# A new list of step order and step engines for a linear-attention and SoLU feed-forward kernel on one Trainium2 core

## The chip, the core and the metric

The kernel runs on one core of a Trainium2 chip, in one launch. The metric is the device time of that launch in microseconds. The inputs are drawn once; q, k and v are 8 batches of 8 heads, 576 rows and 64 columns in float32, the weights are 512 by 1024 and 1024 by 512, and the output is 4608 by 512.

## The reference

```python
q_s = softmax(q, axis=-1)                 # over a head's 64 columns
k_s = softmax(k, axis=2)                  # over the 576 rows of the sequence
kv  = einsum('bhsd,bhse->bhde', k_s, v)
x   = einsum('bhsd,bhde->bhse', q_s, kv)  # then heads side by side: 4608 x 512
h   = x @ w_in
sm  = softmax(h, axis=-1)
solu = h * sm
ln  = (solu - mean) / sqrt(var + 1e-6) * g_ln
out = ln @ w_out
```

## The kernel before

The work is cut into named streams, each a Python generator. One call of a stream emits one step: one instruction or a few, on engines that the code fixes or, where the code says `on(default)`, on an engine that the list can choose. A constant, ORDER (L21 to L85), is the whole schedule: a string of names, and `in_turns` (L643) calls the streams in the order of the string. The n-th mention of a name is that stream's n-th step, counted here from 0, so h1[14] is the fifteenth mention of h1. `*3` repeats a name, `.v` asks for VectorE. In a step without `on(...)` the suffix does nothing. Each engine executes its instructions in the order in which the string emits them, and an instruction that waits holds up all that stands behind it on its engine; the DMA queue of SyncE, which carries every transfer, works the same way.

The streams, with their lines:

- LQ, LK, LV, V: loads of q, k and v of a batch (L177 to L218). V has a second step that casts to the tile with a column of ones (L190, ScalarE or VectorE).
- w0 to w3 and y0 to y3: the rows of w_in and w_out. Two loads of 512 KB, then L239 (ScalarE), L241 and L243 (VectorE) which turn the 64-bit words into float32, then a sum of magnitudes (L256 or L287, ScalarE). W and Z then scale the weights and split them into two float16 parts: W[0] to W[3] find the scale of w_in, W[4] to W[11] are L268 on ScalarE and L270 on VectorE in turn; Z does the same for w_out, with L309 and L311, Z[0] being L292 to L297 and Z[19] the last L311.
- K of a batch (L335): maxima over rows (L346, L348, L351 on VectorE; transposes L322 and L329 on TensorE), subtraction (L357, L362, chosen), Exp (L359, L364), the product with v (L376, L381), the scale (L384 to L390, L157, L164 to L168) and the float16 block matrix (L403 to L407).
- Q..a, Q..c, R (L412 to L478): softmax of q (L424, L426, L428, L431 to L435, L437), a split into two float16 parts (L440, L442) and a transposing DMA.
- x of a row tile (L494): 16 or 32 small matmuls, then L516 on ScalarE and L518 on VectorE.
- h of a row tile (L522): 24 matmuls of 512 columns in six steps (L533), L540 and L542, Exp (L546), four one-column operations am, pi, p, ph (L550 to L559, GpSimd by default), the product with its sum (L562 on VectorE, L564), u (L567 on ScalarE, L569 on VectorE), the transposing DMA (L572), the square (L576, ScalarE) and four more one-column operations (L580 to L589).
- o of a row tile (L594): 24 matmuls in four steps (L607), the copy out of the accumulator (L615 on VectorE or L617 on ScalarE), the store.
- P: four matmuls on zeros (L662), whose result nobody reads.

There are 36 row tiles. The accumulator of h has two buffers, so the matmuls of one tile can start only after L576 of the tile two before it; o has one buffer, and x, K and the scales share three. TensorE's order is a mix: steps of h, o, x and K stand between each other as the string says.

Of the kernel before, what the change touches and what calls it, by code (L numbers as in the profile page):

```python
# [17 lines left out]
P = 128  # L18

BUFS = 12, 4, 2  # L20
ORDER = (  # L21
# [63 lines left out]
)  # L85


@with_exitstack
def linear_attention_solu_ffn(ctx: ExitStack, tc: tile.TileContext, q, k, v, w_in, w_out, g_ln, out):

# [633 lines left out]
```

## Time and profile before

| quantity | value |
|---|---|
| time of the runs, median of 3 | 489.39 us (489.34 to 490.88) |
| span of the profiled execution, first to last instruction | 488.0 us |
| TensorE, busy share of the span | 93% |
| VectorE | 74% |
| ScalarE | 57% |
| GpSimd | 42% |
| mean granted clock of TensorE | 0.972 |
| DMA, mean | 154 GB/s |

The profiled execution's own time is not listed apart from its span; against the median of the runs the span is 1.39 us shorter. A busy TensorE is not TensorE at its peak, because matmuls overlap; its useful work is better counted in matmuls.

### The profile page before, as it was taken

The numbers are of one execution on the slowest core, as the hardware profiler recorded it, in microseconds if no ns is written. First come the engines' busy times: TensorE is split into PE (matmuls) and PEld (weight loads), VectorE is DVE, ScalarE is ACT, GpSimd is POOL, SyncE is SP. The second block draws the span as 40 slices with busy tenths as digits, with TensorE's granted clock in tenths as the row PEclk, the third lists the DMA queues.
The fourth block names the chain that finished last, engine by engine and source line by source line (L and its number), as shares of the span: only waits on it lengthen the run. The fifth ranks groups of instructions, "written<-read, shape, count | busy, mean of one in ns | idle before, by whom it ended". The sixth has DMA issues, their size and how long they took to land.

```text
span 488.0 us, 8325 instructions
## 1 busy us (share of the span) xinstructions
PE 453.0 (93%) x3150; PEld 223.0 (46%) x3150; DVE 359.2 (74%) x610; ACT 280.2 (57%) x463; POOL 202.7 (42%) x303
## 2 busy tenths in 40 slices
PE   5748576999999999999999999999999999999997
PEld 1324242445555444454445445544554444444444
DVE  3989999987889897887897885987786754544220
ACT  1577698777648546765574656654645544533322
POOL 3312666478526636742564457254231431221120
PEclk9868987999999999999999999999999999999999
DMA  8899589279875967569659947794225544151162
GB/s 263 274 208 297 205 178 219 63 151 249 198 194 128 247 105 172 135 147 253 131 130 217 246 100 164 140 253 103 66 43 109 107 109 88 39 113 19 47 152 84
DMA packets 159240, 74.99 MB, mean 154 GB/s; under 512 B 127840, under 2 KB 152672, under 8 KB 159200
## 3 DMA queue, kind: packets, MB, share of 16 engines
q1 hardware_dynamic: 159200, 74.47, 64.4%
q8 instruction: 24, 0.39, 0.3%
q14 instruction: 16, 0.13, 0.1%
HBM read 36.70 MB, written 9.44 MB: 95 GB/s over the span
## 4 chain that ended last, share of the span: by engine, by line
PE 78%; DVE 12%; ACT 4%; DMA 3%; issue 2%; SPq 0%; POOL 0%; DVEq 0%; ACTq 0%
PE o L607 36%; PE h L533 34%; PE x L509 3%; PE kv L376 3%; DMA kr<-in_k_dram 2%; DVE u L569 2%; DVE top L540 1%; DMA v<-in_v_dram 1%; DVE wi L270 1%; ACT u L567 1%; DVE gw L243 1%; DVE h L562 1%; ACT e L576 1%; DVE qnmx L424 1%; PE kv L381 1%
## 5 line engine op out<-in xcount | busy, mean ns | idle before, releaser
L533 PE MATMUL h<-wi,xT 128*128 128x512 f16 x864 | 203.9, 385 | 11.2 <-ACT e L576 9.8
L607 PE MATMUL o<-wo,uT 128*128 128x512 f16 (+1 forms) x888 | 197.7, 373 | 0.8 <-DVE os L615 0.8
L533 PEld LDWEIGHTS <-xT 128*128 128x128 f16 x864 | 84.2, 99 | 111.6 <-issue 18.5
L607 PEld LDWEIGHTS <-uT 128*128 128x128 f16 x888 | 85.3, 98 | 96.7 <-issue 1.1
L540 DVE TENSOR_REDUCE top<-h 128x1 f32<-128x1024 f32 x36 | 43.9, 1219 | 43.3 <-PE h L533 43.3
L569 DVE SCALAR_TENSOR_TENSOR u<-h,nmu,u 128x1024 f16<-128x1024 f32 x36 | 45.9, 1276 | 15.0 <-ACT u L567 14.9
L576 ACT ACTIVATE e<-h,nmu 128x1024 f32<-128x1024 f32 x36 | 40.0, 1111 | 20.9 <-DVE u L569 20.8
L562 DVE SCALAR_TENSOR_TENSOR h<-h,ph,e 128x1024 f32<-128x1024 f32 x36 | 46.2, 1283 | 7.2 <-POOL ph L559 6.2
L542 ACT ACTIVATE nm<-top,hs 128x1 f32<-128x1 f32 x32 | 9.4, 294 | 61.8 <-DVE top L540 61.8
L567 ACT ACTIVATE u<-h,nmu 128x1024 f16<-128x1024 f32 x36 | 40.0, 1111 | 1.0
L442 POOL TENSOR_TENSOR qhl<-qm,qhl 128x1024 f16<-128x1024 f32 (+1 forms) x12 | 24.9, 2075 | 34.9 <-ACT qhl L148 22.0
L546 ACT ACTIVATE e<-h,nm,hs 128x1024 f32<-128x1024 f32 x32 | 38.4, 1200 | 0.8
L556 POOL TENSOR_TENSOR p<-pi,mone 128x1 f32<-128x1 f32 x36 | 22.6, 627 | 37.9 <-DVE pi L553 36.5
L550 POOL TENSOR_SCALAR am<-nm 128x1 f32<-128x1 f32 x17 | 7.6, 449 | 70.0 <-ACT nm L542 69.9
L426 POOL TENSOR_TENSOR qm<-qm,qnmx 128x1024 f32<-128x1024 f32 (+1 forms) x14 | 25.1, 1799 | 24.0 <-DVE qnmx L424 20.5
L437 POOL TENSOR_TENSOR qm<-qm,qrec 128x1024 f32<-128x1024 f32 (+1 forms) x13 | 24.8, 1911 | 12.9 <-DVE qrec L435 6.7
L589 POOL TENSOR_TENSOR r<-var,mhalf 128x1 f32<-128x1 f32 x36 | 20.3, 565 | 23.9 <-DVE var L586 23.2
L564 ACT ACTIVATE nmu<-s 128x1 f32<-128x1 f32 x36 | 7.3, 202 | 38.3 <-DVE h L562 35.1
L518 DVE SCALAR_TENSOR_TENSOR xT<-x,xT 128x512 f16<-128x512 f32 x36 | 24.3, 679 | 3.2 <-ACT xT L516 3.2
L615 DVE TENSOR_SCALAR os<-o,rr 128x512 f32<-128x512 f32 (+1 forms) x18 | 12.9, 719 | 17.9 <-PE o L607 17.6
L509 PEld LDWEIGHTS <-bd 128*64 128x64 f16 x640 | 18.3, 113 | 15.7 <-issue 11.6
L617 ACT ACTIVATE os<-o,rr 128x512 f32<-128x512 f32 x19 | 13.0, 683 | 18.6 <-PE o L607 14.2
(130 smaller groups left out, 564.0 us busy)
## 6 DMA issues: line engine op xcount, KB each, us to landing
v<-in_v_dram SPq DMA_DIRECT2D x32, 256.0 KB, 3.9
out_dram<-os SPq DMA_DIRECT2D x31, 256.0 KB, 3.0
km<-in_k_dram SPq DMA_DIRECT2D x7, 1024.0 KB, 6.6
qm<-in_q_dram SPq DMA_DIRECT2D x7, 1024.0 KB, 6.2
w_in<-in_moe_w_in_dram SPq DMA_DIRECT2D x8, 512.0 KB, 5.8
w_out<-in_moe_w_out_dram SPq DMA_DIRECT2D x8, 512.0 KB, 5.6
out_dram<-os SPq DMA_DIRECT2D x10, 128.0 KB, 2.4
qm<-in_q_dram SPq DMA_DIRECT2D x2, 512.0 KB, 4.3
```

The source lines that it names most:

```text
L426: on(nc.gpsimd).tensor_tensor(x, x, wide(nmx), op=ALU.add)
L437: on(nc.gpsimd).tensor_tensor(x, x, wide(rec), op=ALU.mult)
L442: on(nc.gpsimd).tensor_tensor(lo, x, hi, op=ALU.subtract)
L509: nc.tensor.matmul(acc[j * D : (j + 1) * D, pr, cols], t[:, s, 2 * pr + j], qT[:, 2 * pr + j, cols], start=(s == 0), stop=(s == 1),)
L533: nc.tensor.matmul(h[:, ns], xT[:, t, kc], wi[:, s, kc, ns], start=(i == 0), stop=(i == len(terms) - 1))
L540: nc.vector.tensor_reduce(top, h, axis=AX.X, op=ALU.max, negate=True)
L546: nc.scalar.activation(e, h, AF.Exp, bias=nm, scale=hs, accum_out=z)
L562: nc.vector.scalar_tensor_tensor(h, h, ph, e, op0=ALU.mult, op1=ALU.mult, accum_out=s1)
L567: nc.scalar.activation(u[:, 0], h, AF.Identity, bias=nmu)
L569: nc.vector.scalar_tensor_tensor(u[:, 1], h, nmu, u[:, 0], op0=ALU.add, op1=ALU.subtract)
L576: nc.scalar.activation(e, h, AF.Square, bias=nmu, accum_out=s2)
L607: nc.tensor.matmul(o, uT[:, j, f], wo[:, s, f, cols], start=(f == 0 and j == 0 and s == 0), stop=(f == NF - 1 and j == 1))
```

## The change

Only ORDER is replaced. Buffers, tiles, operations and their number stay; both lists hold the same 1728 steps, and every stream has the same number of mentions. What changes is the order in which the steps are emitted, and which engine a choosable step takes. The new list was searched with a model that limits the transfers in flight and counts the collisions of GpSimd and VectorE.

The suffix `.v` stands 163 times in the old list and 661 times in the new one, but most of the added ones are on steps that cannot choose. Counted by engine, the choosable steps that differ most are:

| step | before | after |
|---|---|---|
| copy of o: L617 ScalarE / L615 VectorE | 19 / 18 | 25 / 12 |
| cast of v (L190): ScalarE / VectorE | 21 / 11 | 24 / 8 |
| q minus its maximum, whole (L426): GpSimd / VectorE | 12 / 3 | 14 / 1 |
| q times the reciprocal, whole (L437): GpSimd / VectorE | 12 / 3 | 11 / 4 |
| k minus its maximum (L357): GpSimd / VectorE | 7 / 9 | 8 / 8 |
| am (L550), pi (L553), first z (L580) on GpSimd | 17, 18, 18 | 19, 20, 23 |
| second z (L583), var (L586) on GpSimd | 20, 21 | 16, 20 |

The heads of the two lists:

```diff
-    "LQ0*2 LK0*3 V03 w3 Q0a K0*4 Q0a*2 K0 P*4 K0 Q0b w3 V00 V03.v K0 Q0c K0 Q0b Q0a w3 w0 K0 w3 V00 Q0b "
-    "w3 V01 K0.v Q0b K0 w0 V01.v K0.v w0*2 LV0 K0 w0 K0.v Q0c*2 V02 w3 Q0a.v V02 w2 K0 w2 P*3 K0 Q0a.v "
-    "Q0b P*2 K0 w2 w1 Q0b w0 w1 K0 w2 Q0c Q0a Q0b K0*2 w2 K0 w1 K0 w1 K0*2 w1 K0 Q0a w2 LK1 Q0b K0*2 w1 "
-    "K0 Q0c.v V11 LK1 K1 P x0 x1 W K1 W y0 Q0c V12 K1 y1 W V11 x0 W x0 W Q0c K1 P h0 W*4 h0 K1 y0 h0 Q0c "
-    "W*2 h0 y1 W LQ1 y0 V10 S0.v h0*2 V12 y0 V13 K1 x1 h0 K1 x1 h0 x2 y0 h0 K1 y1 h1 x3 K1 y2 y1 h1 y2 "
-    "x2 h0 h1 x3 h1 h0 h0.v y0 h0 x2 K1 Q1a h0*4 h1 Q1c h1 y1 K1 y3 K1*2 LV1 y3 h2 Q1a*2 V10 h2 K1 V13 "
-    "h2 h1 h2 Q1a LQ1 h2 h1 Q1a.v h2 h1.v LQ1 K1 h0 y2 h1 K1*2 x3 Q1a K1 h1 h2*2 h1 y1 y2 h1 LG y3 Q1a "
-    "K1 h1 y2 K1 V21 K1 h2 Q1a y3 h1 LK2 h1 K1 h1 h2 h3 y2 h2*2 K1*2 h2 y3 K1 h3 h2 h1 y3 K1 h2 Z h3 K1 "
...
+    "LQ0*2 Q0a.v LK0 Q0b Q0a Q0b.v LK0 V03 K0*2 Q0a LK0 K0 w3 V03 K0 w3 Q0a P Q0b P K0 V00.v P Q0a Q0c.v "
+    "P w3 K0*3 Q0b.v w0*2 V00 V01 w3 Q0c K0 w3 w0 V01 K0.v w0 K0 K0.v K0 Q0c Q0a w0 Q0a K0.v Q0c V02 LV0 "
+    "V02 Q0b.v K0*2 w2 K0 Q0c.v K0 Q0b w2 V11 w2 K0 w1 K0 w0 Q0b w1 w2 w1 K0*2 Q0a LK1 Q0b.v w2 K0 P w1 "
+    "K0 K0.v K0*2 LK1 K0 w2 w1 K1 w3 w1 K1*2 V13 K1 W y1 x0 P W K1 Q0c W K1 x0 Q0c y1 V13 W K1 x1 x0 W*5 "
+    "K1 W*3 LG y1 y0 h0.v h0 y0 h0.v y1 h0 y0 h0 S0 h0 P K1 y0 Q0c x1 x3 V11 x2 h0 y0 h0 h0.v y0 x1 LQ1 "
+    "h0 P V10 h1 h0 x3 h1*2 LQ1 h0 x2 V10 Q1a K1 h1 V12 y2 h1 h0 y2 y1 Q1a h0 LV1 h0.v LV2 y3*2 h1 K1 V12 "
+    "K1 h0.v x2 h0 P y2 Q1c Q1a h1.v LQ1 K1 x3 Q1a y2 h1 K1 y3 h1 h2.v h2*3 K1 h1*2 h2 V22.v h2 Q1a.v Q1a "
+    "y1 K1*2 V21.v K1 h1 Q1c P h1*2 Q1a h2 K1*2 h1.v Q1a LK2 h2.v h1.v h2 K1 h1 P h2 h3 y2 h2.v y2 h3 "
...
```

Decoded for VectorE, between W[3] (the scale of w_in is known) and h1[14] (L569 of tile 1):

- Only the old list has there: K1[3] (L348), K1[4] (L351), S0 (L485), ph of tile 0 (L559), am of tile 1 (L550), y2[4] (L243), K1[20] (L157), y3[3] (L241). The first two stand ahead of W[3] in the new list, S0 and the two one-column operations are on GpSimd there, and the last three come after h1[14].
- Only the new list has there: am of tile 0 (L550).

From W[3] on to Z[19], only the old list has K1[3], K1[4], S0, ph of tile 0, am of tile 1, K2[2] (L346), K2[3] (L348), K2[4] (L351) and R1[0] (L424 on the rest of q); only the new list has am and the second z of tile 0.

On GpSimd, the old list has K1[9] (L357) behind p of tile 0 while ph of tile 0 stands on VectorE; the new list has ph of tile 0 ahead of K1[9], both on GpSimd. On TensorE, the order of streams up to h3 holds the same work; five of the eleven P steps stand ahead of K0's product with v in the old list after the first four, and none in the new one, which has P steps behind h0, x2, h1, K1[17] and K1[19] instead. On SyncE, the load V11 stands ahead of w1's loads in the new list and far behind them in the old one.

Between the last step of a tile's h and the first of the tile that takes over its accumulator, the new list has the least TensorE work at these places: h30 to h32 (24 matmuls of h31, 18 of o25), h26 to h28 (24 of h25, 18 of o20, K7[5]), h12 to h14 (24 of h13, 12 of o8, two x, K4[5] and K4[7]), h24 to h26 (24 of h22, 24 of o17), h11 to h13 and h31 to h33. In the old list the least is at h15 to h17 (24 of h16, 6 of o9, two x).

120 rows, old and new, of the table ORDER are left out of this document.

## The prediction, made before the change was run

> **What bounds the kernel now.** I read the page first, for the stretches that are not full.
>
> ```profile
> span 488.0 us, 8325 instructions
> PE 453.0 (93%) x3150; PEld 223.0 (46%) x3150; DVE 359.2 (74%) x610; ACT 280.2 (57%) x463; POOL 202.7 (42%) x303
> PE   5748576999999999999999999999999999999997
> DVE  3989999987889897887897885987786754544220
> ```
>
> The fortieths are 12.2 us long. TensorE (PE) is full from the eighth on, from about 85 us; before that VectorE (DVE) is full and TensorE is not. Two waits views, TensorE from 85 to 485 us and VectorE from 41 to 85 us, say how full (us in total, times, longest):
>
> ```profile
> PE h L533 <- ACT e L576: 1.7, 3, 0.9
> PE o L607 <- DVE os L615: 0.8, 1, 0.8
> ```
>
> ```profile
> DVE u L569 <- ACT u L567: 0.9, 1, 0.9
> DVE gw L241 <- ACT gw L239: 0.4, 1, 0.4
> ```
>
> After 85 us TensorE waits 1.7 + 0.8 = 2.5 us in 400, so a new order can win no more than that there, and can lose any amount. From 41 to 85 us VectorE waits 1.3 us: it is the bound of that stretch, and TensorE gets what it leaves over. The timeline shows what the matmuls of the first tiles wait for (start, length, then the wait before it):
>
> ```profile
> 41.69 5.44 PE L533 MATMUL h<-wi,xT 128*128 128x512 f16 x22 [0.91 <-ACT wi L268]
> 52.14 4.49 PE L533 MATMUL h<-wi,xT 128*128 128x512 f16 x20
> 63.55 1.21 DVE L540 TENSOR_REDUCE top<-h 128x1 f32<-128x1024 f32 x1
> 74.35 1.28 DVE L569 SCALAR_TENSOR_TENSOR u<-h,nmu,u 128x1024 f16<-128x1024 f32 x1
> 75.67 1.11 ACT L576 ACTIVATE e<-h,nmu 128x1024 f32<-128x1024 f32 x1 [1.35 <-DVE u L569]
> 76.92 3.57 PE L533 MATMUL h<-wi,xT 128*128 128x512 f16 x8 [4.04 <-ACT e L576]
> 93.76 0.74 DVE L311 SCALAR_TENSOR_TENSOR wo<-gw,gs,wo 128x512 f16<-128x512 f32 x1
> ```
>
> The first h starts at 41.69. Tile 1 has its matmuls done at 56.6 (52.14 + 4.49), its maximum is begun only at 63.55, its u on VectorE at 74.35, and at 76.92 its accumulator is handed to h3: twenty microseconds in VectorE's queue. The last part of w_out is ready at 94.5 (93.76 + 0.74).
>
> **The change part by part.** First, VectorE's queue from W[3] to h1[14], the step of 74.35. Rows of the groups view (after the bar busy us and mean ns of one):
>
> ```profile
> L243 DVE SCALAR_TENSOR_TENSOR iw<-w_in,iw 128x1024 int32<-128x1024 int32 x4 | 4.9, 1222 | 0.1
> L351 DVE TENSOR_TENSOR ktop<-ktop,kr 64x512 f32<-64x512 f32 x8 | 5.6, 700 | 0.2
> L348 DVE TENSOR_TENSOR ktop<-khalf 128x256 f32<-128x256 f32 x16 | 7.9, 497 | 0.2
> L241 DVE TENSOR_SCALAR gw<-gw 128x1024 int32<-128x1024 int32 x4 | 2.8, 688 | 0.4 <-ACT gw L239 0.4
> L157 DVE TENSOR_REDUCE top_kv<-kv 128x1 f32<-128x128 f32 x8 | 2.2, 281 | 0.0
> L550 DVE TENSOR_SCALAR am<-nm 128x1 f32<-128x1 f32 x19 | 4.0, 209 | 2.0 <-ACT nm L542 1.9
> L346 DVE TENSOR_TENSOR khalf<-km 128x512 f32<-128x512 f32 x16 | 11.0, 686 | 4.0 <-DMA km<-in_k_dram 3.8
> L424 DVE TENSOR_REDUCE qnmxr<-qr 128x8 f32<-128x512 f32 x4 | 2.7, 680 | 0.0
> ```
>
> The old list alone has K1[3] 0.50, K1[4] 0.70, y2[4] 1.22, K1[20] 0.28, y3[3] 0.69 there: 3.4 us; its am of tile 1 and the new one's of tile 0 cancel; S0 and ph, two one-column operations, add some 0.2 each if taken at am's 0.21. That is 3.8, of which I take **3.6 us**, since L348 by its usual row is nearer 0.42 and the small ones run into each other. A second anchor agrees: up to the last part of w_out the new list is shorter by K1[3], K1[4], S0, ph, am, K2[2] 0.69, K2[3] 0.50, K2[4] 0.70 and R1[0] 0.68, less two one-column operations: again 3.7 or so. At Z[0] between the two it is shorter by 0.9 only, because the postponed steps come there; TensorE then has h3, two x and five of h5's six steps ahead of the first o, about 11 us, which covers them. If it did not, 0.9 would be the gain. So this term lies between -0.9 and -3.7. K1[3] and K1[4] now stand ahead of W[3], where VectorE waits anyway for the last sums of w_in on ScalarE (L256); without that cover they cost 1.2 at the first h.
>
> Second, collisions. Timeline, GpSimd (POOL) beside VectorE:
>
> ```profile
> 52.73 2.39 POOL L357 TENSOR_TENSOR km<-km,kb 128x1024 f32<-128x1024 f32 x1 [0.51 <-DMA v<-in_v_dram]
> 52.82 2.32 DVE L559 TENSOR_TENSOR ph<-p,hs 128x1 f32<-128x1 f32 x1
> 60.19 2.36 POOL L357 TENSOR_TENSOR km<-km,kb 128x1024 f32<-128x1024 f32 x1
> 60.43 3.19 DVE L243 SCALAR_TENSOR_TENSOR gw<-w_out,gw 128x1024 int32<-128x1024 int32 x1
> ```
>
> ```profile
> L559 DVE TENSOR_TENSOR ph<-p,hs 128x1 f32<-128x1 f32 x10 | 3.7, 369 | 2.3 <-POOL p L556 2.2
> ```
>
> A one-column ph takes 2.32 us beside K1's subtraction and ends with it; the ten of its group together take 3.7, so the other nine average 0.15. L243 takes 3.19 instead of 1.22. These two cost 2.16 + 1.97 = 4.1 us, on the full engine. In the new list ph of tile 0 is on GpSimd ahead of that subtraction, so the first collision goes. y1[4], the slow L243, still meets K1[9], by my walk through the queue in its last half microsecond. Bounds: 0 if new meetings cost as much as the old ones, -4.1 if all go. I take **-2.2**, the one that the list excludes.
>
> Third, what may wait newly. ScalarE has y3[2] (L239) ahead of K1[14], K1[14] ahead of K1's product, and VectorE has K1[18] ahead of h1[14]: a late y3 holds h3.
>
> ```profile
> w_out<-in_moe_w_out_dram SPq DMA_DIRECT2D x8, 512.0 KB, 5.6
> 19.00 6.63 SPq L228 DMA_DIRECT2D w_in<-in_moe_w_in_dram  x4
> 31.46 1.17 ACT L239 ACTIVATE iw<-w_in 128x1024 f32<-128x1024 f32 x1 [1.86 <-DMA w_in<-in_moe_w_in_dram]
> ```
>
> y3 can be issued when y1[4] is done, and lands 5.6 us later, 6.6 if the second pair of w_in is the measure (the last four issues end at 25.6, at 31.46 ScalarE has the words). Between y1[4] and the use VectorE has u (1.28), x2, Q1c, h1's maximum (1.21), x3, Q1a's sums and y2[3] (0.69): seven items of about one microsecond, an estimate from the three quoted, so it just fits: 0 to +3, I take **+1.0**. The same rows hold for the start: V11 (256 KB) now stands ahead of w1's loads, but these wait on w0[4], which the new list brings about 1 us earlier; I take the first h at its old time, within a microsecond.
>
> Fourth, after 85 us.
>
> ```profile
> 443.04 10.36 PE o L607 x48
> 231.80 1.11 ACT L576 ACTIVATE e<-h,nmu 128x1024 f32<-128x1024 f32 x1 [1.35 <-DVE u L569]
> 224.62 1.23 DVE L540 TENSOR_REDUCE top<-h 128x1 f32<-128x1024 f32 x1 [1.01 <-PE h L533]
> 233.06 2.10 PE L533 MATMUL h<-wi,xT 128*128 128x512 f16 x9 [0.89 <-ACT e L576]
> ```
>
> A matmul takes 10.36/48 = 0.216 us. From the end of h15 (224.4) to the release (233.0) passed 8.5 us, the tightest handover of the old list, and it cost 0.89. The tightest in the new list is h30 to h32, 42 matmuls or 9.1 us; then 42 and a K step (9.7), 10.3, 10.4 and twice 11. So the new list has no place under 8.5, but six under 11. Bounds -2.5 (no wait left) to +5; I take **+0.6**. Six copies of o move from VectorE to ScalarE:
>
> ```profile
> L615 DVE TENSOR_SCALAR os<-o,rr 128x512 f32<-128x512 f32 x16 | 12.0, 749 | 12.1 <-PE o L607 11.8
> L617 ACT ACTIVATE os<-o,rr 128x512 f32<-128x512 f32 x19 | 13.0, 683 | 18.6 <-PE o L607 14.2 <-issue 1.9 <-DMA out_dram<-os 1.4
> ```
>
> 6 x 0.75 = 4.5 us less for VectorE, 4.1 more for ScalarE, both hidden by matmuls after 85 us; so are the other exchanges between GpSimd and VectorE. Most of the added `.v` choose nothing. Costed at nothing, and if the cover were gone a copy would cost its 0.7 once per o. The tail is the same: the last tile in two halves, copied and stored.
>
> Sum: -3.6 - 2.2 + 1.0 + 0.6 = **-4.2**, against the profiled span 488.0 a span of 483.8. The runs' median of 489.39 lies 1.39 above that span, so 485.2.
>
> **The rivals.** About 0.3% (1.5 us) is what a measurement of this kernel can tell from no change: 487.9 to 490.9.
>
> *Stalls at the handover of h (slower).* One mechanism: at the six tight places the chain from L540 to L576 takes longer than the matmuls that cover it. With a chain of 11.5 us the shortfalls are 2.4 + 1.8 + 1.2 + 1.1 + 0.5 + 0.5 = 7.5, and the time 492.7. It decides from about 11.2 us (shortfall 5.7), where the new list is slower than the bound. For it: tile 1's chain lasted from 56.6 to 76.8. Against: the only forced one took 8.5, and two of the six places lie after 360 us, where VectorE is half idle.
>
> *A cold clock in the first tiles (no difference).* Granted clock by stage (last columns: PEclk, DMA share, GB/s):
>
> ```profile
> 27.00:40.50 13.50, 9.42 (x90) 6.01 (x91) 11.48 (x28) 9.96 (x18) 3.73 (x3) 0.50 1.06 259
> 40.50:61.00 20.50, 14.08 (x91) 6.60 (x90) 19.98 (x23) 14.44 (x21) 9.64 (x8) 1.00 0.79 237
> 74.50:81.50 7.00, 4.58 (x11) 1.57 (x11) 6.08 (x10) 5.72 (x11) 5.96 (x12) 0.51 1.07 226
> ```
>
> [...] The new list takes five P steps (20 matmuls) from ahead of K0's product. If h0 runs half speed for its first 6.8 us, it has 16 matmuls done instead of 24 in 5.2, and ends 2 us later; another 3.4 us at half in h1 costs 1.7. Together +3.7: 488.9. [...] Against the rival: x, the scale and a P still stand ahead of h0, and the new list has P steps between h0, h1 and K1, where the old one had none and lost the clock from 74.5 to 81.5.
>
> *All collisions go and nothing waits (faster still).* -3.6 - 4.1 = -7.7: 481.7. For it: the list was made with these collisions priced. Against: y1[4] still stands where K1[9] runs.
>
> *The list does nothing*: the gain of VectorE at Z[0] is 0.9, and if the first o hangs on that, 488.5. It goes with the cold clock as one case.
>
> **How the numbers follow.** Forecast 0.54 (own range 483.0 to 487.4), faster still 0.18, no difference 0.15, handover stalls 0.13. Faster by over 0.3%: 0.54 + 0.18 = 0.72; same 0.15; slower 0.13. The range 481.7 to 489.5 takes in the faster rival and both no-difference cases and leaves out the stalls and some of what lies below.
>
> **What would show it.** Right: VectorE full from 41 to about 80 us; the wait of h3 on L576 ending near 71 to 73 instead of 76.9; no one-column operation of 2 us on VectorE between h0 and h2; the last L311 at 88 to 91; TensorE full from about 80. Wrong: a PEclk of 0.5 across 41 to 48; waits of h on L576 above 3 us after 85; L239 of y3 waiting for its DMA by more than 2 us.

## The result, and the profile after

| quantity | before | after |
|---|---|---|
| time, median | 490.13 us (4 runs, 489.34 to 491.33) | 475.39 us (4 runs, 473.71 to 477.42) |
| ratio, 95% interval | | 0.9694 (0.9658 to 0.9730) |
| profiled execution: time, span | listed only by its span, 488.0 us | 477.42 us, 475.6 us |
| mean granted clock of TensorE | 0.972 | 0.964 |

The new list is 14.7 us faster by the medians; 4.2 was forecast, and the time lies below the range. The profiled execution of the new kernel is the slowest of its four runs, so the two profiles differ by 488.0 - 475.6 = 12.4 us. Medians and ratios are those of undisturbed runs; of one experiment (Z[1]'s place) the profiled execution ran disturbed, so no profile of it is used.

The page of the new kernel, the lines that answer to those of before and the granted clock:

```profile
span 475.6 us, 8323 instructions
PE 445.4 (94%) x3150; PEld 224.3 (47%) x3150; DVE 342.7 (72%) x596; ACT 283.5 (60%) x472; POOL 208.8 (44%) x308
PE   4367989999999999999899999999999999999997
DVE  3989999979988898768888877656787655531610
PEclk9555999999999999999999999999999999999999
```

TensorE is nearly full from the fifth fortieth on (48 us; P steps are among it), not from the eighth. But it was as full afterwards in the old kernel; what changed there is not to be seen in these digits. The waits of TensorE from 85 to 485 us, as before (us in total, times, longest):

```profile
PE wide L339 <- DVE col L335: 1.3, 1, 1.3
PE h L543 <- ACT e L586: 0.8, 2, 0.6
```

2.1 us of waits where there were 2.5. Now the timeline of TensorE. Line numbers of the new kernel are 10 higher (h is L543, o is L617, x is L519):

```profile
43.53 6.46 PE L543 MATMUL h<-wi,xT 128*128 128x512 f16 x24
59.67 5.34 PE L543 MATMUL h<-wi,xT 128*128 128x512 f16 x24 [0.71 <-ACT e L586]
71.64 4.48 PE L543 MATMUL h<-wi,xT 128*128 128x512 f16 x20 [1.42 <-ACT e L586]
78.78 4.48 PE L543 MATMUL h<-wi,xT 128*128 128x512 f16 x20 [0.57 <-ACT e L586]
83.09 5.34 PE L617 MATMUL o<-wo,uT 128*128 128x512 f16 x24
454.66 17.49 PE L617 MATMUL o<-wo,uT 128*128 128x512 f16 x104
```

and the first and last rows of o in the old kernel:

```profile
87.84 2.75 PE L607 MATMUL o<-wo,uT 128*128 128x512 f16 x12
459.71 24.83 PE L607 MATMUL o<-wo,uT 128*128 128x512 f16 x138
```

The first h starts 1.8 us later than in the old profile (43.53, 41.69), h3 5.3 earlier (71.64, 76.92), the first o 4.8 earlier, and the last matmul ends at 454.66 + 17.49 = 472.15 instead of 484.54, 12.4 earlier. So the gain has two parts, and one lies where TensorE was full already. These marks cut each profile into stages. To compare them, the matmuls' own time, their mean distance from start to start at full clock in the two profiles, is taken off: 0.216 us for each of h and o, 0.109 for a transpose, 0.0305 for one of K's product, 0.025 for one of x, nothing for P. From the first h to the first o the new list has done 29.3 us of work, the old list 27.6 (20 of h5's matmuls instead of 8, but K1's eight transposes ahead of the first h); from there 387.5 and 390.1 us are left. What remains is called lost. The last 48 matmuls of o have 256 columns and come 0.109 apart, so the zero of this scale is off by some 5 us in the last stage and only differences count.

| profile | first h at | first h to first o | lost in it | first o to last matmul | lost in it |
|---|---|---|---|---|---|
| old kernel | 41.69 | 46.16 | 18.6 | 396.70 | 6.6 |
| new kernel | 43.53 | 39.56 | 10.2 | 389.06 | 1.6 |

8.3 us come from the stage between the first h and the first o, 5.0 from the long full stage, and 1.0 more was lost ahead of the first h (the other 0.9 of its 1.8 are the transposes moved there). Over the profiles below with an unchanged start, 18.6 to 19.6 us were lost from the first h to the first o in the old list (five), 9.7 to 10.7 in the new one (four).

### The profile page after: what moved, and what is told of

Read it like the earlier page. It is cut to its first block, busy times and chain, and to the rows that moved or that the text cites. A ratio compares the mean times of both kernels' runs of the same rounds, so it can differ in the third digit from the quotient of the medians.

```text
span 475.6 us, 8323 instructions
## 1 busy us (share of the span) xinstructions
PE 445.4 (94%) x3150; PEld 224.3 (47%) x3150; DVE 342.7 (72%) x596; ACT 283.5 (60%) x472; POOL 208.8 (44%) x308
## 4 chain that ended last, share of the span: by engine, by line
PE 77%; DVE 7%; DMA 7%; ACT 4%; issue 2%; SPq 2%; POOL 1%; DVEq 0%; ACTq 0%
PE o L617 35%; PE h L543 33%; PE x L519 3%; PE kv L386 3%; DMA qT<-qhl 3%; DMA w_in<-in_moe_w_in_dram 2%; DMA km<-in_k_dram 2%; DVE top L550 1%; DVE gw L253 1%; PE wide L339 1%; DVE u L579 1%; PE kv L391 1%; DMA v<-in_v_dram 1%; PE turned L332 1%; ACT e L586 1%
## 5 line engine op out<-in xcount | busy, mean ns | idle before, releaser
L543 PE MATMUL h<-wi,xT 128*128 128x512 f16 x864 | 200.7, 381 | 3.5 <-ACT e L586 3.5
L617 PE MATMUL o<-wo,uT 128*128 128x512 f16 (+1 forms) x888 | 198.6, 373 | 0.0
L543 PEld LDWEIGHTS <-xT 128*128 128x128 f16 x864 | 84.5, 98 | 103.9 <-issue 6.3
L617 PEld LDWEIGHTS <-uT 128*128 128x128 f16 x888 | 86.0, 98 | 96.8
L550 DVE TENSOR_REDUCE top<-h 128x1 f32<-128x1024 f32 x36 | 43.9, 1218 | 31.4 <-PE h L543 31.1
L572 DVE SCALAR_TENSOR_TENSOR h<-h,ph,e 128x1024 f32<-128x1024 f32 x36 | 46.2, 1286 | 10.8 <-POOL ph L569 6.7
L586 ACT ACTIVATE e<-h,nmu 128x1024 f32<-128x1024 f32 x36 | 40.0, 1110 | 15.2 <-DVE u L579 15.0
L452 POOL TENSOR_TENSOR qhl<-qm,qhl 128x1024 f16<-128x1024 f32 (+1 forms) x13 | 26.3, 2020 | 34.3 <-ACT qhl L158 28.2
L627 ACT ACTIVATE os<-o,rr 128x512 f32<-128x512 f32 (+1 forms) x25 | 16.8, 674 | 29.1 <-PE o L617 20.4
L447 POOL TENSOR_TENSOR qm<-qm,qrec 128x1024 f32<-128x1024 f32 (+1 forms) x12 | 22.4, 1868 | 23.2 <-DVE qrec L445 18.2
L436 POOL TENSOR_TENSOR qm<-qm,qnmx 128x1024 f32<-128x1024 f32 (+1 forms) x15 | 29.5, 1969 | 3.7 <-DVE qnmx L434 3.7
L563 POOL TENSOR_SCALAR pi<-am 128x1 f32<-128x1 f32 x20 | 6.5, 323 | 51.6 <-DVE am L560 47.6
L599 POOL TENSOR_TENSOR r<-var,mhalf 128x1 f32<-128x1 f32 x36 | 21.0, 583 | 12.9 <-DVE var L596 12.2
L386 PE MATMUL kv<-vm,km 128*64 128x65 f32 x512 | 18.5, 234 | 6.0 <-ACT km L369 6.0
```

Source lines behind the costliest of these rows:

```text
L386: nc.tensor.matmul(o, km[:, h + i, c], vm[:, h + i, c], start=(h == 0 and c == 0), stop=False)
L436: on(nc.gpsimd).tensor_tensor(x, x, wide(nmx), op=ALU.add)
L452: on(nc.gpsimd).tensor_tensor(lo, x, hi, op=ALU.subtract)
L543: nc.tensor.matmul(h[:, ns], xT[:, t, kc], wi[:, s, kc, ns], start=(i == 0), stop=(i == len(terms) - 1))
L550: nc.vector.tensor_reduce(top, h, axis=AX.X, op=ALU.max, negate=True)
L572: nc.vector.scalar_tensor_tensor(h, h, ph, e, op0=ALU.mult, op1=ALU.mult, accum_out=s1)
```

## The experiments

All but one edit only ORDER. Unless said otherwise an experiment's ratio is to the old kernel on the same chip, and one per cent is 4.9 us.

**Two halves, swapped.** `head_new` is the new list up to o1's first matmuls, then what is left in the old order; `tail_new` is the reverse. `after_again` is the new kernel once more.

```diff
-ORDER of one list
+its first 337 (new) or 344 (old) steps, then all other steps in the order of the other list
```

> The new list up to the step ahead of o1's first matmuls (337 steps), then the old list's order for all that is left. Theory (two separate gains: VectorE's queue and its collisions in the first 85 us, and fewer changes between 512-column matmuls and small ones afterwards): only the first gain is there, 7 us, so 483 against 490.1. Rival A (the whole gain comes from the start): 476. Rival B (my prediction's terms were right for the start and the rest comes later): 485 to 486. The start's timeline should show h3 begin at 71 to 72, as in the new kernel.

> The old list up to the step ahead of o1's first matmuls (344 steps), then the new list's order for all that is left. Theory: only the second gain is there, 5 us, so 485 against 490.1. Rival A (the whole gain comes from the start): 489 to 490, since TensorE waits only 2.5 us after 85 us in the old kernel. If the two parts add, the gains of this run and of the one with the new start together make 14 to 15 us; if they overlap, less.

> The new kernel once more, for comparison on this chip: 475.4.

Measured: `head_new` 483.31 us, ratio 0.9842 (0.9809 to 0.9875); `tail_new` 486.33, 0.9886 (0.9852 to 0.9920); `after_again` 476.48, 0.9685 (0.9643 to 0.9727). The two gains, 1.58% and 1.14%, make 2.72% or 13.4 us, against 3.1%: they add, but for a rest of some 2 us that the intervals allow. The first and last o of `tail_new`:

```profile
90.67 2.75 PE L617 MATMUL o<-wo,uT 128*128 128x512 f16 x12
454.70 27.42 PE L617 MATMUL o<-wo,uT 128*128 128x512 f16 x150
```

From 90.67 to 482.12 are 391.45 us, where the old order of the same remaining work takes 396.70: 5.25 us won in the stage in which the prediction allowed 2.5 at most. In `head_new` 38.96 us pass from the first h to the first o, and then 396.43 (8.9 lost, 2.3 more than in the old kernel; 1.9 of it are waits of TensorE, 4.4 after 85 us against 2.5, and that they come from steps which the new start puts off is not shown).

**The price of a stretch of small matmuls.** The rows that led there, TensorE in the old kernel at full clock:

```profile
180.74 1.67 PE L533 MATMUL h<-wi,xT 128*128 128x512 f16 x7
182.25 0.60 PE L322 MATMUL turned<-ident,ktop 128*128 128x128 f32 x4
182.69 1.46 PE L607 MATMUL o<-wo,uT 128*128 128x512 f16 x6
...
189.54 0.64 PE L509 MATMUL x<-qT,bd 128*64 128x128 f16 x16
190.11 1.47 PE L607 MATMUL o<-wo,uT 128*128 128x512 f16 x6
191.51 0.64 PE L509 MATMUL x<-qT,bd 128*64 128x128 f16 x16
```

Read them from start to start, since the printed length of a group contains its last matmul's end. Seven matmuls of h ahead of four transposes take 182.25 - 180.74 = 1.51 = 7 x 0.216, the transposes 0.44 = 4 x 0.11: no surcharge. Six of o ahead of an x take 191.51 - 190.11 = 1.40, 0.10 over 6 x 0.216, and the 16 of x 0.57. The timeline shows no wait for this. In the new kernel one x stands against a whole product of K:

```profile
352.05 0.64 PE L519 MATMUL x<-qT,bd 128*64 128x128 f16 x16
352.52 2.04 PE L386 MATMUL kv<-vm,km 128*64 128x65 f32 x64
354.49 0.68 PE L391 MATMUL kv<-vr,kr 64*64 64x65 f32 x16
355.10 1.47 PE L617 MATMUL o<-wo,uT 128*128 128x512 f16 x6
```

16 of x take 0.47 here, where K's follow instead of o's, and 0.57 above. From o0 on the x and K matmuls stand in 37 stretches of their own between h's and o's in the old list, in 15 in the new one. `after_split` is the reverse: the same work in 60.

```diff
                             start=(s == 0), stop=(s == 1),
                         )
+                if pr < NP - 1 and bb == groups[0][0]:
+                    yield
         yield
```

> The new list with the matmuls of 27 x groups (x7 to x35 without x9 and x13) each issued in four parts of 4 or 8 instead of at once, each part behind the next step of large matmuls; where two groups stood side by side their parts still meet. From o0 on, the stretches of small matmuls between large ones rise from 15 to 60. All work is the same. Theory (0.25 us per stretch): 45 x 0.25 = 11 us more, 486 to 487 against 475.4, and TensorE shows as busy as before. Rival (only waits cost): 475.4, or some tenths more where an x comes late for its h.

Measured: 488.20 us, 0.9928 (0.9900 to 0.9956), 11.7 us above `after_again`, 11.9 by the ratios. TensorE in it, at full clock:

```profile
188.18 0.41 PE L522 MATMUL x<-qT,bd 128*64 128x128 f16 x8
188.53 1.47 PE L622 MATMUL o<-wo,uT 128*128 128x512 f16 x6
189.92 0.41 PE L522 MATMUL x<-qT,bd 128*64 128x128 f16 x8
```

Eight of x take 0.35 and sixteen took 0.57, so each costs 0.0275, and 0.57 - 16 x 0.0275 = 0.13 is fixed; the six of o again take 1.39, 0.09 over. Together 0.23 us for a stretch, be it 8 or 16 of x. With 45 stretches more that makes 10.4; 11.8 to 13.5 were lost more from the first o to the end (13.35 against 1.6 and, in `after_again`, -0.2), with 2.8 us of waits where the new kernel had 2.1. For the new list 22 stretches less make 5.1, and 5.0 to 6.8 were won there. Some of that is waits: 2.5 us in the old kernel, 2.1 in the new one, 0.5 in `after_again`, 1.6 in `tail_new`. Without them 4.4 to 4.8 remain, 0.20 to 0.22 for each stretch.

Going the other way, in the old list, was harder. `before_merge`, `before_merge2` and `before_merge3` move lone matmuls next to the following small ones, which leaves 29, 25 and 26 of the 37 stretches:

```diff
-x12[0] (19 steps) x11[0]
+x12[0] x11[0]
-K3[15] (8 steps) K3[16] (12 steps) K3[17]
+K3[15] K3[16] K3[17]
```

(the second pair in the latter two only).

> The old list, in which the matmuls of ten x groups that stood alone between 512-column matmuls (x12, x14, x15, x18, x20, x22, x24, x28, x32, x33) are moved later, next to the matmuls of the next x group; nothing else moves (for x32 its copy as well). From o0 on, the stretches of small matmuls between large ones fall from 37 to 29. Theory (each such stretch costs TensorE 0.25 us without any wait being shown): 8 x 0.25 = 2.1 us less, 488.0 against 490.1. Rival (order does not matter while nothing waits): 490.1, or above by the waits of h on x that the later x groups may bring.

> The old list with twelve stretches of small matmuls fewer from o0 on (37 to 25), chosen so that no wait is laid bare: x12, x14, x15, x22, x28 and x32 moved next to the x that follows, and the first halves of the products of K3 to K7 moved later, next to the last part (K3[15], K3[16], K4[15], K5[15], K5[16], K6[15], K7[15]). The groups x20 and x33, whose move uncovered waits of h in the first such run, stay. Theory (a stretch costs TensorE 0.2 us by itself): 12 x 0.2 = 2.4 us less from the first o to the end, 394.3 there against 396.7, and 488.5 in all against 491. Rival (what is saved comes back as waits, as in the first such run): 396.5 or more there, 491.

> The old list with x12, x14, x15, x22, x28 and x32 next to the x that follows, and K3[15], K3[16], K4[15], K6[15], K7[15] next to the last part of their products: 11 stretches of small matmuls fewer (37 to 26). K5's product stays, whose move laid bare a wait of 1.3 us of o for its copy. Theory: the stretches save 0.17 to 0.2 us each, 1.9 to 2.2 us, and no new wait over 0.3 us appears: 394.5 to 394.9 from the first o to the end against 396.7. Rival (waits fill whatever is freed, wherever it is): 396 or more.

Measured: 491.73 us, 1.0006 (0.9980 to 1.0033); 491.66, 1.0010 (0.9976 to 1.0044); 489.28, 0.9950 (0.9921 to 0.9979). From the first o to the end 396.85, 396.37 and 394.98 us, 396.70 in the old kernel. The first two were misses. Where x20 stood in the old kernel, and the same h in `before_merge`:

```profile
244.38 0.64 PE L509 MATMUL x<-qT,bd 128*64 128x128 f16 x16
245.51 1.89 PE L533 MATMUL h<-wi,xT 128*128 128x512 f16 x8 [0.49 <-ACT e L576]
```

```profile
248.20 1.89 PE L533 MATMUL h<-wi,xT 128*128 128x512 f16 x8 [1.06 <-ACT e L576]
```

The x had filled part of the wait of h for its accumulator; taken away, the wait grew by 0.57, all that x takes. In `before_merge2` K5's product had covered the copy of an o:

```profile
257.35 1.02 PE L607 MATMUL o<-wo,uT 128*128 128x512 f16 x4 [1.32 <-ACT os L617]
```

With both left in place, `before_merge3` won 1.72 us in that stage, 0.16 for each of 11 stretches, just under the 0.17 to 0.2 expected, with the same waits as the old kernel to 0.1 us. So the stretches cost about what they seem to, 0.16 to 0.25 by the way it is measured, and joining them pays only where nothing hides behind them.

**The start: the clock.** The rival in its strongest form: what the new list gains is that its P steps keep the clock up. The P steps of the one list are put at the places of the other.

```diff
-P behind K0[19], x0, h0[5], x2, h1[5], K1[17], K1[19]
+P ahead of K0[15] (three), K0[16] (two), x0 and h0
```

> The new list with its eleven P steps where the old list has them: 4 ahead of K0[5], 3 ahead of K0[15], 2 ahead of K0[16], one ahead of x0 and one ahead of h0; none behind h0, x2, h1 and K1's product. Theory (VectorE's queue sets the end of the start, so the clock of TensorE in it hardly matters): within 1.5 us of the new kernel, 475 to 477. Rival (the P steps between the first tiles keep the clock, and that is the gain): the clock drops again near 61 to 65 and 75 to 85, the first o comes 4 to 6 us later, 480 to 482.

> The old list with its eleven P steps where the new list has them: 4 ahead of K0[5], then one each behind K0[19], behind x0, behind h0[5], ahead of h1[0], behind h1[5], behind K1[17] and behind K1[19]. Theory (VectorE's queue): within 1.5 us of the old kernel, 489 to 491.5. Rival (clock): the clock stays full from the first h on and 4 to 6 us are gained, 485 to 486.

Measured: 477.03 us, 0.9683 (0.9639 to 0.9728), and 492.91, 1.0006 (0.9979 to 1.0033). Lost from the first h to the first o: 10.5 in the one, 18.9 in the other, as in the kernels that they come from, though h3's 20 matmuls took 6.16 us in `after_P_old` (at 70.07) and 4.48 in the new kernel. So the places of P are not the gain. The clock is not without a price, though. In the old kernel h2 and h3 ran in part at half clock (0.50 granted from 61.0 to 64.4 and from 74.7 to 81.5 us), each after a long wait:

```profile
60.68 7.03 PE L533 MATMUL h<-wi,xT 128*128 128x512 f16 x24 [4.05 <-ACT e L576]
```

From the first h to the first o, 18 matmuls of h start 0.38 to 0.43 us apart at half clock instead of 0.216 in the old profile, 5 in the new one; that is 3.71 us against 1.05, and so 2.7 of the 8.3 us. It goes with the waits (4.05 ahead of h2, 4.04 ahead of h3; 0.71 and 1.42 in the new kernel); that the waits bring it on was not tested by itself.

**The start: one part of the new list undone.** `after_ph_dve` puts ph of tile 0 back on VectorE; `after_vec_old`, `after_act_old` and `after_Z1_old` restore the old order of VectorE, ScalarE and TensorE around u of tile 1 (with ScalarE's order h2's maximum on VectorE, h2[6], moves too); `after_all_old` does all four.

```diff
-h0.ph (GpSimd) K1[9]
+K1[9] h0.ph (VectorE)
-h1[14] K1[20] y2[4] y3[3]
+y2[4] K1[20] y3[3] h1[14]
-y3[2] h1[12] h1[13] h2[6] h2[7]
+h2[6] h2[7] h1[12] y3[2] h1[13]
-h3[3] h3[4] h3[5] Z[1]
+Z[1] h3[3] h3[4] h3[5]
```

> The new list with one step changed: ph of tile 0 (L569) back on VectorE, behind K1[9] instead of ahead of it, as the old list has it, so that it meets K1[9]'s subtraction on GpSimd. Theory (a collision on the full engine costs what it lasts): ph takes 2.0 to 2.4 us, the first o comes 2 us later, 477.5. Rival (hidden, since VectorE's queue makes it up or the path lies elsewhere): 475.4.

> The new list with three VectorE steps back ahead of h1[14], as in the old list: y2[4] (L253), K1[20] (L167), y3[3] (L251). Theory (the steps on VectorE ahead of u of tile 1 count in full): u 1.22 + 0.28 + 0.69 = 2.2 us later, the time lost from the first h to the first o rises from 10.4 (10.24 and 10.61 in two runs of the new kernel) to 12.6, the time to 478 against 476. Rival (another queue is later anyway, so order on VectorE is free within 2 us): 10.4, 476.

> The new list with ScalarE's order at u of tile 1 as in the old list: the maximum and Exp of h2 (L550, L556) ahead of h1's product, and y3's conversion (L249) ahead of u (L577). Theory (ScalarE is nearly as full as VectorE, so its order counts): VectorE waits 2 us and more for u, 12.5 to 13.5 us lost from the first h to the first o, 478 to 479 against 476. Rival (ScalarE has slack): 10.4, 476.

> The new list with the transpose Z[1] on TensorE ahead of h3's last three steps, as in the old list, instead of behind h3. Theory (h3's second half then waits for the scale of w_out): TensorE waits 3 us at Z[1], the first o comes 1.5 to 2.5 us later, 477.5 to 478.5 against 476. Rival (h5 waits for h3's predecessor anyway): 476.

> The new list with all four undone at once: ph of tile 0 on VectorE behind K1[9], the three VectorE steps, ScalarE's order, Z[1]'s place. Theory (they add): 10.4 + 2.4 + 2.2 + 2.5 + 2 = 19.5 us lost from the first h to the first o, near the old kernel's 18.6, and 483 to 485. Rival (they hide behind each other): 13 to 15 us lost, 478 to 480.

| kernel | median us | ratio (interval) | lost, first h to first o |
|---|---|---|---|
| new kernel, again | 476.48 | 0.9685 (0.9643 to 0.9727) | 10.6 |
| ph on VectorE | 478.78 | 0.9733 (0.9701 to 0.9765) | 12.8 |
| VectorE's order | 479.86 | 0.9764 (0.9738 to 0.9789) | 13.7 |
| ScalarE's order | 479.67 | 0.9776 (0.9759 to 0.9793) | 14.3 |
| Z[1]'s place | 477.42 | 0.9730 (0.9708 to 0.9753) | |
| all four | 482.70 | 0.9821 (0.9799 to 0.9844) | 16.7 |

By the ratios they cost 2.4, 3.9, 4.5 and 2.2 us, 12.9 in sum; together they cost 0.0136 or 6.7 us. With that of the new kernel the intervals are 2.2 to 2.6 us wide to each side, so the second and third are clear of noise. The first is clear only by its runs, which all lie above those of the new kernel on the same chip (477.82 to 480.79, 475.37 to 477.20), and by its profile; Z[1]'s place is not shown to cost anything. The sum carries the new kernel's error four times; the profiles, whose lost time scatters by 1 us in one list, say the same: three parts lose 2.2, 3.1 and 3.7 more than `after_again`, 9.0 in sum, and all four 6.1. They hide behind each other, and no part alone is "the" cause. With all four, 16.7 us are lost where the old start loses 18.6; what the rest hangs on was not tested. What ScalarE's order does, in `after_act_old` (VectorE, then h3):

```profile
70.00 1.28 DVE L579 SCALAR_TENSOR_TENSOR u<-h,nmu,u 128x1024 f16<-128x1024 f32 x1 [1.95 <-ACT u L577]
72.57 7.43 PE L543 MATMUL h<-wi,xT 128*128 128x512 f16 x20 [3.28 <-ACT e L586]
```

VectorE waits 1.95 us for ScalarE, the square that releases the accumulator comes later, TensorE stands still for 3.28 instead of 1.42, and these 20 matmuls of h3 take 7.43 instead of 4.48, more than the wait grew by. That is the length with 14 of them 0.427 us apart, as at half clock in the old profile, and the others 0.216 (an estimate from these lengths).

**The start: parts put into the old list.** `before_queue` has VectorE's order changed (with ph and S0 on GpSimd, and K2[2] to K2[4] and R1 behind Z[19]); `before_queue2` leaves K2 and R1, and changes ScalarE's order and Z[1]'s place too; `before_queue3` adds the new places of P.

> The old list with VectorE's order changed alone: y2[4], K1[20] and y3[3] behind h1[14]; K2[2], K2[3], K2[4] and R1[0] (with R1[1]) behind Z[19]; S0 and ph of tile 0 on GpSimd, ph so ahead of K1[9]. TensorE's order, the P steps and all else stay as in the old list. Theory (the start's 7 us are VectorE's queue and its collision with K1[9]): h3 begins 1.22 + 0.28 + 0.69 + 0.2 + 2.3 = 4.7 us earlier, and most of it reaches the first o: 4 to 5 us less, 486 against 490.5. Rival (the clock: TensorE at half speed for 3.4 us at 61 and 7 to 10 us at 75 to 85 in the old list, never after the first h in the new one): the first h tiles still fall into the half clock, and 1 us at most is gained.

> The old list with VectorE's order changed as in the earlier run (y2[4], K1[20], y3[3] behind h1[14]; S0 and ph of tile 0 on GpSimd), but K2 and R1 left where they were, and now ScalarE's and TensorE's too: h2's maximum and Exp and y3's conversion (L239) behind u of tile 1 (L567), and h3's last three steps ahead of the transpose Z[1]. Theory (with VectorE's queue shorter, ScalarE's queue and Z[1]'s place were late next): no wait of 2.3 us of VectorE on u, h3 28 to 30 us after the first h (35.2 in the old kernel, 32.3 in the earlier run), 14 to 15 us lost from the first h to the first o instead of 18.6, and no more lost after: 486 to 487 against 491. Rival (a further thing is late next): 32 us, 490 to 491.

> The old list with VectorE's, ScalarE's and Z[1]'s order changed as in the second such run, and its P steps where the new list has them. In that run h0 took 7.58 us and h3 8.02 us instead of 5.4, at half clock. Theory (the clock counts once the queues are shorter): h3 at full clock, 2 to 3 us less lost from the first h to the first o than its 18.5, 487 to 488.5. Rival (the clock hardly matters here either, as in the two runs that moved the P steps alone): 18 to 18.5 us lost, 490.

Measured: 491.68 us, 0.9995 (0.9968 to 1.0022); 490.37, 0.9973 (0.9947 to 1.0000); 493.41, 1.0022 (0.9992 to 1.0052). Three misses. In `before_queue`, VectorE and then TensorE:

```profile
72.81 1.28 DVE L569 SCALAR_TENSOR_TENSOR u<-h,nmu,u 128x1024 f16<-128x1024 f32 x1 [2.33 <-ACT u L567]
75.38 4.84 PE L533 MATMUL h<-wi,xT 128*128 128x512 f16 x12 [4.53 <-ACT e L576]
81.28 0.32 PE L154 MATMUL wide_out<-ident,m_out 128*128 128x128 f32 x1 [1.06 <-DVE m_out L297]
```

From the first low part of w_in on VectorE (L270, at 43.26 and in the old kernel at 41.86) to u of tile 1 passed 27.2 us without that wait instead of 32.5 (72.81 - 2.33 - 43.26, 74.35 - 41.86), the 5 us that were meant to go; 2.33 of them became a wait for ScalarE, and Z[1], in the middle of h3, then waited for VectorE. h3 came 32.3 us after the first h (35.2 in the old kernel, 28.1 in the new one), and of the 2.1 us won up to the first o, all were lost after it (2.6). `before_queue2` mends that wait, but h0 and h3 took 7.58 and 8.02 us where h2 took 5.34, as with 11 and 13 of their 24 matmuls at half clock (an estimate from 0.427 us apart against 0.216):

```profile
43.95 7.58 PE L533 MATMUL h<-wi,xT 128*128 128x512 f16 x24 [0.76 <-ACT wi L268]
77.18 8.02 PE L533 MATMUL h<-wi,xT 128*128 128x512 f16 x24 [4.50 <-ACT e L576]
```

and in both later runs x5, which stands behind Z[1] there, made h5 wait 0.7 for ScalarE and 0.9 for VectorE. With P moved (`before_queue3`) h3 still took 7.48, and 19.0 were lost. Why the old list takes no part of the new start with profit isn't settled beyond this: each run shows another step that came late next.

**The first h.** In the new profile K1[4] on VectorE met GpSimd's L452 and held up the scale of w_in:

```profile
37.75 2.23 POOL L452 TENSOR_TENSOR qhl<-qm,qhl 128x1024 f16<-128x1024 f32 x1 [9.38 <-ACT qhl L158]
38.10 2.43 DVE L361 TENSOR_TENSOR ktop<-ktop,kr 64x512 f32<-64x512 f32 x1
```

```diff
-K1[4] W[2] K1[5] W[3] K1[6] K1[7] h0[0]
+W[2] W[3] K1[4] K1[5] W[5] K1[6] h0[0] K1[7]
```

> The new list with K1[4] (L361) behind W[3], K1[5] behind it, K1[6] behind W[5] and K1[7] behind h0's first step, so that K1[4] no longer meets GpSimd's L452 ahead of the scale of w_in. Theory (this collision held the first h back by 1.7 us): the scale is known 1.7 us earlier, the first h starts near 41 instead of 41.3 to 43.5, and 1 to 1.7 us are gained: 474 against 475.4. Rival (something else, x1 or the words of w_in, holds the first h): 475.4.

Measured: 476.00 us, 0.9682 (0.9638 to 0.9725), the same as `after_again`. L361 took 0.95 and the first h came at 41.25, but 40.63 us passed from there to the first o, so 0.9 of the 1.6 us was left at the first o and none in the end. No version tried beats the new kernel by more than can be measured.

## Why the prediction was wrong in size

- **The failed step: "After 85 us TensorE waits 1.7 + 0.8 = 2.5 us in 400, so a new order can win no more than that there."** It took the absence of waits for the absence of loss. The order won 5.0 us there in the profiles and 5.25 with the old start, of which waits are 0.4 and 0.9; the rest is 22 stretches of small matmuls fewer, at some 0.2 each. The numbers lay in the profile of before: the start-to-start times at 190.11 and 191.51 were not read. The term of +0.6 stands against -5.0. That is 5.6 of the 8.2 us by which the profiles moved more than forecast (12.4, 4.2); 3.5 are the start, -8.3 where the sum had -3.6 - 2.2 + 1.0 = -4.8, less the 1.0 lost ahead of the first h.
- **VectorE's queue to h1[14], -3.6:** right in direction, and the queue did bind: undoing its three steps costs 3.9 by the ratios, 3.1 in the profile, where their durations make 2.2. But the sum had no term for ScalarE's order (4.5 if undone) nor for the half clock that goes with the waits of h (2.7 between the two profiles), and the parts overlap. Z[0] was said to come 0.9 earlier by VectorE's steps, 3.1 with the collision; it (L302, L292 in the old kernel) began 33.65 us after the first h instead of 39.66, 6.0 earlier. VectorE in the new kernel, with the parts of w_out behind it, and in the old one:

```profile
77.18 0.15 DVE L302 TENSOR_REDUCE g<-gl 128x4 f32<-128x8 f32 x1
81.41 5.65 DVE L321 SCALAR_TENSOR_TENSOR wo<-gw,gs,wo 128x512 f16<-128x512 f32 x8
```

```profile
81.35 0.15 DVE L292 TENSOR_REDUCE g<-gl 128x4 f32<-128x8 f32 x1
```

- **Collisions, -2.2:** right; putting ph back costs 2.4, 2.2 in the profile. Its rows in `after_ph_dve`, and y1[4] in the new kernel:

```profile
51.41 1.21 DVE L434 TENSOR_REDUCE qnmx<-qm 128x16 f32<-128x1024 f32 x1
51.87 2.36 POOL L367 TENSOR_TENSOR km<-km,kb 128x1024 f32<-128x1024 f32 x1
52.53 1.72 DVE L569 TENSOR_TENSOR ph<-p,hs 128x1 f32<-128x1 f32 x1
```

```profile
53.75 2.36 POOL L367 TENSOR_TENSOR km<-km,kb 128x1024 f32<-128x1024 f32 x1
55.36 1.83 DVE L253 SCALAR_TENSOR_TENSOR gw<-w_out,gw 128x1024 int32<-128x1024 int32 x1
```

  y1[4] still meets K1[9], as forecast, for 0.6 us over its 1.22 and not the 2.0 of before: 1.4 more won, which the -2.2 left out.
- **y3 late, +1.0:** did not happen; L249 of y3 shows no wait for its load:

```profile
63.66 1.15 ACT L249 ACTIVATE gw<-w_out 128x1024 f32<-128x1024 f32 x1
```

- **First h "within a microsecond":** 1.8 later in the profile, but over nine profiles with an unchanged start it came at 41.53 to 43.90 in the old list and 41.28 to 43.53 in the new one. The cover named for K1[4] failed (the collision above), and it made no difference that outlasts the start.
- **The rivals:** the handover of h costs 0.8 us in all, so the stalls stayed out, as argued. The cold clock came in part, at half (0.50 granted) from 11.7 to 45.8 us, and h0 took 6.46 where h2 took 5.34; h1 ran at full clock (1.00 granted). No run shows the 6.8 us at half clock in h0 and the 3.4 in h1 that its sum takes: in the new profile half clock covers h0's first 2.3 us (43.53 to 45.8), and stretches of 3.4 and 6.8 us stand at 61.0 and 74.7 in the old one, in h2 and around h3's start. Its price of 2 us for h0 was also mis-added: 16 matmuls in 6.8 us and 8 more at 0.216 end at 8.5, 3.3 after the 5.2. The removed P steps did not turn the sum; what the rival did not see is that less of h runs at half clock in the new kernel, 5 matmuls up to the first o instead of 18, beside shorter waits. "All collisions go" named the nearest time, 481.7, for another reason.
- **Of the signs named:** h3's wait ended at 71.64, in the span of 71 to 73; no one-column step of 2 us stood on VectorE; TensorE was full from 80; the last L311 ended at 87.1, not at 88 to 91, since the queue gained more. A clock of 0.5 across 41 to 48 was named as a sign of a wrong forecast; it stood until 45.8, beside a larger gain.

## What to carry to other kernels

A busy engine without waits can still lose time where the array shape of its matmuls changes (here about 0.23 us for a stretch): read TensorE's rows from start to start, subtract the run's own rate, and count how often the list changes the array shape. Before such stretches are joined, look what each one covers; where a small group fills a wait, moving it wins nothing. A part of a joint rearrangement can cost some 4 us when undone and win nothing when put into the old list, so test it from both lists before its price is believed. A longer wait of TensorE can cost more than its own length, where the matmuls behind it take longer too (7.43 us instead of 4.48 above, behind 3.28 instead of 1.42).

## What the runs showed of the hardware

A stretch of matmuls of another array shape costs about 0.23 us between 512-column ones: 0.10 before it and 0.13 in it. It goes by the shape in the row: x and K's product (128*64, 64*64) pay, transposes (128*128) among h and o don't (7 of h ahead of four transposes take 1.51 us, 7 x 0.216). Inside K's product the change of shape costs too: in the new kernel the first 64*64 matmul starts 0.149 us after the last 128*64 one, where the 128*64 ones come 0.03 apart in the mean. An x followed by K's 128*64 product pays no surcharge between the two: 16 of x take 0.47 us there and 0.57 ahead of o.

Three elementwise steps with two inputs on VectorE took longer beside a GpSimd step: L361 2.43 us beside L452 instead of 0.70, ph 1.72 beside L367 instead of 0.15, L253 1.83 beside L367 instead of 1.22. A maximum, with one input, keeps its 1.21 beside the same subtraction (L434 at 51.41 above). Not every step with two inputs takes longer: L572 in the new kernel keeps its 1.28 beside L367 (at 54.16).

TensorE's half-speed stretches (0.50 granted) last 3.4, 13.7, 3.4 and 6.8 us in the old kernel's profile, from 13.2, 26.9, 61.0 and 74.7 us, and 34.1 in the new one's, from 11.7: multiples of 3.4. In five profiles whose lists are the same up to it, the first h starts at 41.20 (`after_vec_old`) to 43.53 us (the new kernel); whether that is the clock's doing was not tried.
